# Transposing a block's rows further ahead, and two one-bank accumulators, in a fused FFT convolution and two-layer mixture kernel

## The chip, the cores and the metric

One Trainium2 chip; the kernel uses 1 of its cores. The metric is device time in microseconds (us) for one execution. Before the change the median of 3 runs is 4191.43 us (4187.36 to 4192.93).

## What is computed

Three stages on 8 x 3072 tokens of width 256, all in float32 on the host:

```
Y   = rfft(x, axis=1) * (filt_r + 1j*filt_i)           # convolution by FFT
x1  = irfft(Y)                                          # (24576, 256)
e   = argmax(x1 @ w_gate)  ;  g = softmax(...)[e]       # 8 experts, one per token
x2  = g * (relu(x1 @ w1[e]) @ w2[e])                    # w1: 256x1024, w2: 1024x256
h   = x2 @ w_in                                         # 256 -> 2048
out = piecewise(h) @ w_out                              # 0 below -1, (h+1)^2/4 between, h above 1
```

## The kernel before, in words

**Stages.** `Conv` computes the convolution and the routing in the first 640 us or so. `Ffn` computes both dense layers from there to the end, and its first blocks overlap the tail of `Conv`. Only `Ffn` and `slots` are touched by the change.

**Blocks and chunks.** Tokens are sorted by expert into blocks: 41 wide ones of 512 tokens (`NW`) and 17 narrow ones of 256 tokens that always run (up to `SURE` = 58). A block j has 8 steps `("b", j, f)`, one for each 128 columns of the expert's hidden layer. The second layer works on 48 chunks of 512 tokens; a chunk c has 16 steps `("c", c, f)`. `Ffn.run` (L1006) writes all steps into one list. It begins with 60 b steps alone (`lead`, L1012), that is blocks 0 to 6 and half of block 7. After that each chunk's 16 c steps are mixed with the next 8 b steps, the second half of one wide block and the first half of the next; in every second chunk the 8 steps of a narrow block stand between those two halves (L1017), and then c and b steps alternate one by one. Two chunks together make one period of the schedule.

**Order of the work.** `play` (L1062) walks through the list. At step i it issues the first matmuls of the step (`b_in` L870 into a bank h, or `c_in` L936), then what was put into `fill` for i, then the rest of the step's elementwise work, then what was put into `todo` for i + 1, and then the second matmuls of the step that stands 3 places earlier (`LAG` = 3: `b_out` L885 into the accumulator y, or `c_out` L964 into o). Every engine executes its own instructions in the order in which they are issued, so a waiting instruction holds all that stands behind it on its engine.

A c step is a chain over four engines: six matmuls on PE (L936), a clamp on DVE (L940), a square on ACT (L941), a sum on DVE (L943), a cast on ACT (L944, the high part gh) and a subtraction on POOL (L786, the low part gl). `c_out` three steps later needs gh, and from its third matmul on gl. A b step has ACT hh (L872) and DVE hl (L874), and two weight parts wh (ACT, L790) and wl (L786, on DVE for even f, on POOL for odd f).

**How a block gets its rows.** `plan` (L1061) sets for block j, with p[0] the place of its first step in the list: at p[0] - 26 the token numbers are fetched (`gather(j, False)`, L833, tiles ids or idl), at p[0] - 17 the rows (`gather(j, True)`, L840, 4 indirect DMAs on POOL's queue for a wide block, 2 for a narrow one; tiles row, 8 buffers), at p[0] - 9 the rows are scaled by the gate (`scale`, L847, DVE). At p[0] - 7 and p[0] - 4 the two halves (k = 0, 1) of the 256 columns are transposed by PE:

```
for k in range(2):
    at(i - 7 + 3 * k, lambda k=k: self.take(j, k, i - 6 + 3 * k))
```

`take` (L851) writes four 128 x 128 transposes (L858; two for a narrow block) into one bank. In the first blocks that bank comes from the rotating banks h (`h_tile`); once `dense` has run it is the single bank xt (`psx`, one buffer). `halves` then splits the bank: ACT copies it to xh one step later (L790), and DVE subtracts to xl (L786) as `fill` of the step after that. The two tiles xh and xl have 2 buffers each (`xp`), one for each block in work.

**The accumulator.** `b_out` at f = 0 takes a tile y of two banks from a pool with one buffer (`ps_y`) and adds into half d = 0, then d = 1. After f = 7 `b_end` (L892) empties it: for each half an ACT copy to cyh (L898) and a DVE subtraction to cyl (L899). The next block's `b_out` at f = 0 needs the same tile.

`slots` (L627) computes the block table in three phases; phases 1 and 2 run beside the first b steps and take one PSUM bank each, which is xt (`ffn.psx`, passed by the caller).

Of the kernel before, what the change touches and what calls it, by code (L numbers as in the profile page):

```python
# [9 lines left out]
FP32 = mybir.dt.float32  # L10
# [4 lines left out]
ALU = mybir.AluOpType  # L15
AX = mybir.AxisListType
PSUM = bass.MemoryType.PSUM
# [9 lines left out]
CH = 512  # L27
# [87 lines left out]
def width(j):  # L115

    return CH if j < NW else CH // 2
# [506 lines left out]
            yield t  # L624


def slots(tc, a, st, phase, pp=None, side=None):  # L627

    nc, V = tc.nc, tc.nc.vector
    nb, j0, j1 = ((EARLY, 0, NE1), (NB, NE1, NW), (NB, NW, NBLK))[phase]
    J, K, W = j1 - j0, nb - 1, width(j0)
    H, sh = W // 128, W.bit_length() - 1
    whole = phase < 2
    with ExitStack() as ctx:
        p = ctx.enter_context(tc.tile_pool(name="b", bufs=1, side=side))
        cum, off, used = st["cum"], st["off"], st["used"]
        NQ = 2 * K + 4
# [20 lines left out]
            out=out[:, 1:9], data0=one[:, 0:8], data1=x, initial=0.0, op0=ALU.mult, op1=ALU.add  # L660
# [39 lines left out]
        for k in range(2):  # L700
# [3 lines left out]
            out=QJ, in0=QT[:].unsqueeze(2).to_broadcast([8, NQ, J]), in1=oh[:, 0:1].to_broadcast([8, NQ, J]), op=ALU.mult  # L704
        )
        yield
        qs = p.tile([128, NQ, J], FP32, name="qs")
        pp = pp or ctx.enter_context(tc.tile_pool(name="b_ps", bufs=1, space=PSUM, side=side))
        ps = pp.tile([128, CH], FP32, name="xt")[:, : NQ * J].rearrange("p (q j) -> p q j", j=J)
        nc.tensor.matmul(ps, one[:8], QJ, start=True, stop=True)  # L710
        nc.scalar.copy(qs, ps)
        yield
# [4 lines left out]
            out=ecf[:, 1], in0=ecf[:, 1], scalar1=float(CH * (j0 if whole else NW)), scalar2=float(NTOK),  # L717
# [5 lines left out]
        x = p.tile([128, J, H], FP32, name="x")  # L723
        t = p.tile([128, J, H], FP32, name="t")
# [13 lines left out]
class Ffn:  # L738
# [54 lines left out]
    def at(self, i, fn, when=None):  # L793
        (self.todo if when is None else when).setdefault(max(i, self.now), []).append(fn)
# [82 lines left out]
    def b_out(self, j, f):  # L877
        nc, n = self.nc, width(j)
        (hi, lo), (wh, wl) = self.H.pop((j, f)), self.W.pop((j, f))
        if f == 0:  # L880
            self.ACC["b"] = self.ps_y.tile([128, 2, CH], FP32, name="y1")
        acc = self.ACC["b"][:, :, :n]
        for d in range(2):
            for i, (w, x) in enumerate(((wh, hi), (wh, lo), (wl, hi))):
                nc.tensor.matmul(  # L885
                    acc[:, d, :], w[:, 2 + d, :], x,
                    start=(f == 0 and i == 0), stop=(f == 7 and i == 2), skip_group_check=True,
                )
        if f == 7:
            self.b_end(j, acc, n)  # L890

    def b_end(self, j, acc, n):  # L892

        nc, a = self.nc, self.a
        pool = self.cyp if j < NW else self.y1p
        hi, lo = (pool.tile([128, 2, n], F32R, name=x) for x in ("cyh", "cyl"))
        for k in range(2):
            nc.scalar.copy(hi[:, k], acc[:, k])  # L898
            nc.vector.tensor_tensor(out=lo[:, k], in0=acc[:, k], in1=hi[:, k].bitcast(FP32), op=ALU.subtract)  # L899
        if LEADERS <= j < NW:  # L900
            self.CY[j] = (hi, lo, self.rows(self.IDS.pop(j)))
            return
        if j < NW:
            c = slice(CH * j, CH * j + CH)
        else:
            c = nc.sync.value_load(self.st["ec"][0:1, 1, j : j + 1], min_val=0, max_val=NTOK)
            c = bass.ds(c, n)
            ids = self.IDS.pop(j)
            nc.sync.dma_start(a["idc"][c].rearrange("(h p) o -> p (h o)", p=128), ids[:, :2, 0])
        for y, t in (("y1h", hi), ("y1l", lo)):  # L910
            nc.sync.dma_start(a[y][:, :, c], t[:].bitcast(FP32))
# [94 lines left out]
    def run(self):  # L1006
        self.now = -self.LEAD
        sure = SURE
        chunks = [*range(LEADERS, NW), *range(LEADERS), *range(NW, self.nch)]
        wide = [("b", j, f) for j in range(NW) for f in range(8)]  # L1010
        narrow = [[("b", j, f) for f in range(8)] for j in range(NW, sure)]
        lead = 8 * LEADERS + 12  # L1012
        steps, wide = wide[:lead], wide[lead:]
        for m, c in enumerate(chunks):
            more, wide = wide[:8], wide[8:]
            if m >= 2 and m % 2 == 0 and narrow:
                more[4:4] = narrow.pop(0)  # L1017
            n = max(8, len(more))
            for f in range(16):
                steps += [("c", c, f), *more[f * n // 16 : (f + 1) * n // 16]]  # L1020
        assert not wide and not narrow
        pos = {x: i for i, x in enumerate(steps)}
        at = self.at
        fork = pos["c", self.nch - 3, 5]
        at(fork - 16, self.load_used)

        for c in range(self.nch):
            if c < LEADERS or c >= NW:
                at(pos["c", c, 0] - 7, lambda c=c: self.load_c(c))
            for t in range(4 if c < self.nch - 1 else 0):  # L1030
                at(pos["c", c, 15] + 2 + self.LAG + t, lambda c=c, t=t: self.scatter(c, t))
        for j in range(sure):
            p = [pos["b", j, f] for f in range(8)]
            if j <= LEADERS + 1:
                self.plan(p, j, soon=j == 0)
            else:
                self.plan(p, j, ahead=6, lead=8)
        for i in range(16):
            at(lead - 12 + 2 * i, lambda i=i: self.load_w2(i))

        for i in self.play(steps):
            if i == fork:
                self.rest(sure)
            yield i
# [13 lines left out]
                pass  # L1058
        self.todo, self.fill, self.now = keep

    def plan(self, p, j, ahead=3, lead=4, soon=0):  # L1061

        at, i = self.at, p[0] - soon
        at(p[0] - 26, lambda: self.gather(j, False))
        at(p[0] - 17, lambda: self.gather(j, True))
        at(i - 9, lambda: self.scale(j))
        for k in range(2):
            at(i - 7 + 3 * k, lambda k=k: self.take(j, k, i - 6 + 3 * k))
        for q in range(4):
            at(p[2 * q] - ahead - lead, lambda q=q: self.load_w(j, q))  # L1070
        for f in range(8):
            at(p[f] - ahead, lambda f=f: self.split_w(j, f, p[f] - ahead))
# [33 lines left out]
@with_exitstack  # L1106
def tile_fftconv_moe_moe(ctx: ExitStack, tc: tile.TileContext, a: dict):
    st_p = ctx.enter_context(tc.tile_pool(name="st", bufs=1))
    st = {
        "ident": st_p.tile([128, 128], FP32, name="ident"),  # L1110
        "cum": st_p.tile([128, 9, 8], FP32, name="cum"),
        "off": st_p.tile([128, 8, 8], FP32, name="off"),
        "idx": st_p.tile([128, NSC], I32, name="idx"),
        "ec": st_p.tile([1, 2, NBLK], I32, name="ec"),
        "used": st_p.tile([128, 8], FP32, name="used"),
    }
    with tc.manual_schedule(), ExitStack() as end:
        with ExitStack() as c:
            conv = Conv(c, tc, a, st).run()
            for t in conv:  # L1120
                if t == NB * 16 - 1:
                    break
            early = slots(tc, a, st, 0, side="right")
            for t in conv:
                next(early, None)
                if t == NB * 16 + 10:
                    break
            for _ in early:
                pass
            next(conv)  # L1130
            ffn = Ffn(end, tc, a, st)
            blocks = ffn.run()
            for t in conv:
                i = next(blocks)
                for _ in range(3):
                    if i < 0:
                        i = next(blocks)
        ffn.dense(end)
        for k in (1, 2):
            for _ in slots(tc, a, st, k, ffn.psx):  # L1140
                next(blocks)
        for _ in blocks:
            pass
# [59 lines left out]
```

## Time and profile before

| | |
|---|---|
| runs | 4191.43 us median of 3 (4187.36 to 4192.93) |
| profiled execution | 4179.17 us, its span 4177.4 us |
| mean granted TensorE clock | 0.981 of full speed |
| PE busy | 3937.2 us, 94% of the span, 23852 matmuls |
| DVE, ACT, POOL busy | 55%, 48%, 56% |
| DMA | mean 87 GB/s |

PE is busy through nearly the whole span; the other three engines are busy for about half of it. A busy PE time is modelled from the starts of its matmuls, so a wait is seen best in the idle time in front of an instruction, which a row gives in brackets with the instruction that ended it. "PE xt L858 <- DVE xl L786" reads: a matmul of line 858 that writes tile xt stood idle until a DVE instruction of line 786 that writes tile xl ended.

### The profile page before, as it was taken

How to read it: one execution, taken by the hardware profiler on the slowest of the kernel's cores; microseconds unless marked ns; L12 is line 12 of the kernel's file. 1: busy time of each engine (PE TensorE's matmuls, PEld its weight loads, DVE VectorE, ACT ScalarE, POOL GpSimd, SP SyncE). 2: the span in 40 equal slices, each digit the busy share in tenths (PEclk: the TensorE clock that was granted, in tenths of full speed). 3: DMA queues.
4: the chain of work that ended last, by engine and by line, in shares of the span. 5: the costliest groups of instructions: out<-in, count | busy, mean ns of one | idle time of the engine just before them, and what ended most of it. 6: DMA issues, size and time to landing. Idle time of an engine off the chain costs nothing. (4 is left out here: it accounts for less than half of the span.)

```text
span 4177.4 us, 63452 instructions
## 1 busy us (share of the span) xinstructions
PE 3937.2 (94%) x23852; PEld 3345.2 (80%) x23852; DVE 2280.7 (55%) x3643; ACT 2020.2 (48%) x3625; POOL 2334.2 (56%) x2202
## 2 busy tenths in 40 slices
PE   8988887899999999999999999999999999999999
PEld 5655655678888888888888888888888888888888
DVE  5899985564444444444444444444544544454444
ACT  4765664444444444444444444444444444444444
POOL 5777765435555555555555555555555455555555
PEclk9999988999999999999999999999999999999999
DMA  9877764341211211111212111111121121111110
GB/s 298 255 215 220 219 195 132 128 142 56 64 59 56 64 59 58 62 59 60 65 54 64 61 59 60 60 60 60 59 64 59 56 64 39 36 41 35 33 32 26
DMA packets 239321, 364.05 MB, mean 87 GB/s; under 512 B 36544, under 2 KB 160736, under 8 KB 239008
## 3 DMA queue, kind: packets, MB, share of 16 engines
q1 hardware_dynamic: 205280, 300.09, 23.2%
q0 software_dynamic: 25056, 51.36, 4.1%
q10 hardware_dynamic: 8672, 8.48, 0.7%
q8 instruction: 190, 3.11, 0.3%
q14 instruction: 123, 1.01, 0.1%
HBM read 260.52 MB, written 99.30 MB: 86 GB/s over the span
## 5 line engine op out<-in xcount | busy, mean ns | idle before, releaser
L786 POOL TENSOR_TENSOR gl<-m,gh 128x512 fp32r<-128x512 f32 x768 | 997.6, 1299 | 1407.8 <-ACT gh L944 883.2
L941 ACT ACTIVATE m<-m,half 128x512 f32<-128x512 f32 x768 | 556.7, 725 | 1083.3 <-DVE m L940 1083.1
L964 PE MATMUL o<-woh,gh 128*128 128x256 f32 x3084 | 879.5, 285 | 8.1 <-ACT os L957 7.9
L964 PE MATMUL o<-wol,gh 128*128 128x256 f32 x3084 | 871.8, 283 | 1.2 <-DMA wol<-s_w2s 1.2
L964 PE MATMUL o<-woh,gl 128*128 128x256 f32 x3084 | 870.6, 282 | 0.0
L940 DVE TENSOR_SCALAR m<-h 128x512 f32<-128x512 f32 x768 | 529.6, 690 | 520.0 <-PE h L936 456.4
L943 DVE SCALAR_TENSOR_TENSOR m<-h,m 128x512 f32<-128x512 f32 x768 | 530.7, 691 | 487.1 <-ACT m L941 487.1
L944 ACT CAST gh<-m 128x512 fp32r<-128x512 f32 x768 | 476.2, 620 | 606.1 <-DVE m L943 605.3
L874 DVE SCALAR_TENSOR_TENSOR hl<-h,hh 128x512 fp32r<-128x512 f32 (+1 forms) x464 | 284.2, 612 | 661.1 <-ACT hh L872 659.8
L964 PEld LDWEIGHTS o<-woh,gh 128*128 128x128 f32 x3084 | 586.8, 190 | 38.8 <-ACT os L957 12.6
L964 PEld LDWEIGHTS o<-wol,gh 128*128 128x128 f32 x3084 | 588.3, 191 | 27.1 <-DMA wol<-s_w2s 1.5
L936 PE MATMUL h<-cyh,winh 128*128 128x512 f32 x1536 | 608.4, 396 | 1.0 <-PEq L1052 1.0
L936 PE MATMUL h<-cyl,winh 128*128 128x512 f32 x1536 | 606.6, 395 | 0.0
L936 PE MATMUL h<-cyh,winl 128*128 128x512 f32 x1536 | 605.0, 394 | 0.0
L964 PEld LDWEIGHTS o<-woh,gl 128*128 128x128 f32 x3084 | 587.9, 191 | 0.0
L885 PE MATMUL y<-hh,wh 128*128 128x512 f32 (+1 forms) x928 | 343.4, 370 | 21.4 <-DVE cyl L899 21.4
L786 POOL TENSOR_TENSOR wl<-raw,wh 128x512 fp32r<-128x512 f32 x232 | 303.7, 1310 | 96.0 <-ACT wh L790 85.0
L870 PE MATMUL h<-xh,wh 128*128 128x512 f32 (+1 forms) x928 | 341.7, 368 | 5.1 <-DVE hl L874 4.1
L936 PEld LDWEIGHTS h<-cyh,winl 128*128 128x128 f32 x1536 | 289.1, 188 | 67.8
L870 PE MATMUL h<-xh,wl 128*128 128x512 f32 (+1 forms) x928 | 338.2, 364 | 5.1 <-POOL wl L786 4.6
L870 PE MATMUL h<-xl,wh 128*128 128x512 f32 (+1 forms) x928 | 337.6, 364 | 0.0
L885 PE MATMUL y<-hh,wl 128*128 128x512 f32 (+1 forms) x928 | 337.2, 363 | 0.0
(193 smaller groups left out, 6423.7 us busy)
## 6 DMA issues: line engine op xcount, KB each, us to landing
raw<-in_w_dram SPq DMA_DIRECT2D x232, 512.0 KB, 3.4
f<-in_filt_dram SPq DMA_DIRECT2D x72, 384.0 KB, 4.8
xt<-in_x_dram SPq DMA_DIRECT2D x64, 384.0 KB, 5.6
s_z<-zs SPq DMA_DIRECT2D x128, 192.0 KB, 3.7
zt<-s_z SPq DMA_DIRECT2D x64, 384.0 KB, 5.2
s_y<-y SPq DMA_DIRECT2D x128, 192.0 KB, 5.1
cyh<-s_y1h SPq DMA_DIRECT2D x13, 512.0 KB, 3.9
cyl<-s_y1l SPq DMA_DIRECT2D x13, 512.0 KB, 5.1
```

What stands on the lines that cost most here:

```text
L786: eng.tensor_tensor(out=lo, in0=src, in1=hi.bitcast(FP32), op=ALU.subtract)
L870: nc.tensor.matmul(o, w[:, k, :], x[:, k, :], start=i == 0, stop=i == 5)
L874: nc.vector.scalar_tensor_tensor(out=lo, in0=o, scalar=0.0, in1=hi.bitcast(FP32), op0=ALU.max, op1=ALU.subtract)
L885: nc.tensor.matmul(acc[:, d, :], w[:, 2 + d, :], x, start=(f == 0 and i == 0), stop=(f == 7 and i == 2), skip_group_check=True,)
L936: nc.tensor.matmul(ps, w[:, k, 128 * f : 128 * f + 128], x[:, k, :], start=n == 0, stop=n == 5)
L940: V.tensor_scalar(out=m, in0=ps, scalar1=-1.0, scalar2=1.0, op0=ALU.max, op1=ALU.min)
L941: nc.scalar.activation(m, m, ACTF.Square, bias=self.half[:, 0:1], scale=-0.5)
L943: V.scalar_tensor_tensor(out=m, in0=ps, scalar=-1.0, in1=m, op0=ALU.max, op1=ALU.add)
L944: nc.scalar.copy(hi, m)
L964: self.nc.tensor.matmul(self.ACC["c"][t // 2][:, t % 2, :], x[:, 128 * t : 128 * t + 128], w[:, f, :], start=(f == 0 and t % 2 == 0 and n ...
```

## The change

Four edits. (1) `plan` gets a parameter `early`. Blocks 8 and later (up to the last sure one) get (13, 11, 6): rows are gathered at p[0] - 20, scaled at p[0] - 13, and the two halves transposed at p[0] - 11 and p[0] - 6. Blocks 0 to 7 get the default (9, 7, 4), which is what they had, but for the gather of rows, which comes at p[0] - 16 in place of p[0] - 17. (2) The accumulator y becomes two tiles of one bank each. (3) In chunks with a narrow block an empty slot stands before and after the narrow block's 8 steps; the chunk's 18 slots are spread over its 16 c steps, and empty ones are left out. (4) `slots` takes its bank in phases 1 and 2 from the rotating banks h in place of xt.

```diff
-def slots(tc, a, st, phase, pp=None, side=None):
+def slots(tc, a, st, phase, bank=None, side=None):
...
-        pp = pp or ctx.enter_context(tc.tile_pool(name="b_ps", bufs=1, space=PSUM, side=side))
-        ps = pp.tile([128, CH], FP32, name="xt")[:, : NQ * J].rearrange("p (q j) -> p q j", j=J)
+        if not bank:
+            pp = ctx.enter_context(tc.tile_pool(name="b_ps", bufs=1, space=PSUM, side=side))
+            bank = lambda: pp.tile([128, CH], FP32, name="q")
+        ps = bank()[:, : NQ * J].rearrange("p (q j) -> p q j", j=J)
...
         if f == 0:
-            self.ACC["b"] = self.ps_y.tile([128, 2, CH], FP32, name="y1")
-        acc = self.ACC["b"][:, :, :n]
+            self.ACC["b"] = [self.ps_y.tile([128, CH], FP32, name=f"y{d}") for d in range(2)]
+        acc = [t[:, :n] for t in self.ACC["b"]]
...
-                    acc[:, d, :], w[:, 2 + d, :], x,
+                    acc[d], w[:, 2 + d, :], x,
...
         for k in range(2):
-            nc.scalar.copy(hi[:, k], acc[:, k])
-            nc.vector.tensor_tensor(out=lo[:, k], in0=acc[:, k], in1=hi[:, k].bitcast(FP32), op=ALU.subtract)
+            nc.scalar.copy(hi[:, k], acc[k])
+            nc.vector.tensor_tensor(out=lo[:, k], in0=acc[k], in1=hi[:, k].bitcast(FP32), op=ALU.subtract)
...
             if m >= 2 and m % 2 == 0 and narrow:
-                more[4:4] = narrow.pop(0)
+                more[4:4] = [None, *narrow.pop(0), None]
             n = max(8, len(more))
             for f in range(16):
-                steps += [("c", c, f), *more[f * n // 16 : (f + 1) * n // 16]]
+                steps += [("c", c, f), *filter(None, more[f * n // 16 : (f + 1) * n // 16])]
...
-                self.plan(p, j, ahead=6, lead=8)
+                self.plan(p, j, ahead=6, lead=8, early=(13, 11, 6))
...
-    def plan(self, p, j, ahead=3, lead=4, soon=0):
+    def plan(self, p, j, ahead=3, lead=4, soon=0, early=(9, 7, 4)):
         at, i = self.at, p[0] - soon
         at(p[0] - 26, lambda: self.gather(j, False))
-        at(p[0] - 17, lambda: self.gather(j, True))
-        at(i - 9, lambda: self.scale(j))
+        at(p[0] - early[0] - 7, lambda: self.gather(j, True))
+        at(i - early[0], lambda: self.scale(j))
         for k in range(2):
-            at(i - 7 + 3 * k, lambda k=k: self.take(j, k, i - 6 + 3 * k))
+            at(i - early[1 + k], lambda k=k: self.take(j, k, i - early[1 + k] + 1))
...
-            for _ in slots(tc, a, st, k, ffn.psx):
+            for _ in slots(tc, a, st, k, ffn.h_tile):
                 next(blocks)
```

## Rows read from the trace of the kernel before

**Rows 1.** The page: busy us of each engine, share of the span, instructions
```profile
PE 3937.2 (94%) x23852; PEld 3345.2 (80%) x23852; DVE 2280.7 (55%) x3643; ACT 2020.2 (48%) x3625; POOL 2334.2 (56%) x2202
```

**Rows 2.** Waits of PE from 900 us on: us in total, times, longest us
```profile
PE xt L858 <- DVE xl L786: 78.7, 50, 2.8
PE y L885 <- DVE cyl L899: 18.8, 16, 1.2
```

**Rows 3.** Timeline around one second transpose: start us, us, engine, line, operation, [idle before]
```profile
1506.52 0.40 PE L936 MATMUL h<-cyl,winh 128*128 128x512 f32 x1
1506.75 0.39 PE L936 MATMUL h<-cyh,winl 128*128 128x512 f32 x1
...
1507.25 0.69 DVE L940 TENSOR_SCALAR m<-h 128x512 f32<-128x512 f32 x1 [0.73 <-POOL gap L1004]
...
1507.86 0.41 DVE L786 TENSOR_TENSOR xl<-xt,xh 128x256 fp32r<-128x256 f32 x1
...
1508.33 0.44 PE L858 MATMUL xt<-ident,row 128*128 128x128 f32 x2 [1.19 <-DVE xl L786]
```

**Rows 4.** Windows of 3.4 us from a second transpose on: engines' busy us, granted clock
```profile
1083.27:1086.67 3.40, 3.40 (x17) 3.40 (x18) 1.07 (x2) 1.14 (x3) 2.77 (x4) 0.51 0.05 1
...
1239.53:1242.93 3.40, 3.40 (x20) 3.40 (x21) 1.11 (x3) 1.59 (x5) 2.77 (x4) 0.62 0.02 1
...
1395.76:1399.16 3.40, 3.40 (x29) 3.40 (x30) 1.50 (x3) 1.91 (x5) 2.77 (x4) 1.00 0.04 1
...
1550.46:1553.86 3.40, 3.40 (x18) 3.40 (x19) 1.08 (x2) 1.32 (x4) 2.78 (x4) 0.57 0.04 1
...
3499.94:3503.34 3.40, 3.40 (x15) 3.32 (x16) 2.13 (x2) 0.90 (x2) 1.41 (x2) 0.51 0.02 5
```

**Rows 5.** Timeline where a narrow block takes the accumulator after a wide one
```profile
1528.80 0.69 DVE L899 TENSOR_TENSOR cyl<-y,cyh 128x512 fp32r<-128x512 f32 x1 [1.69 <-ACT cyh L898]
...
1530.15 0.69 DVE L899 TENSOR_TENSOR cyl<-y,cyh 128x512 fp32r<-128x512 f32 x1 [0.65 <-ACT cyh L898]
...
1530.89 0.38 PE L885 MATMUL y<-hh,wh 128*128 128x256 f32 x1 [1.17 <-DVE cyl L899]
```

**Rows 6.** Waits of PE from 600 to 900 us
```profile
PE y L885 <- DVE cyl L899: 2.6, 2, 1.4
```

**Rows 7.** Timeline at the first block, POOL and PE
```profile
661.74 0.94 POOL L840 DMA_INDIRECT row<-s_y,idl  x1 [0.30 <-issue]
...
666.45 2.49 POOL L786 TENSOR_TENSOR wl<-raw,wh 128x512 fp32r<-128x512 f32 x2
...
667.77 0.80 PE L870 MATMUL h<-xh,wl 128*128 128x512 f32 x1 [4.59 <-POOL wl L786]
```

**Rows 8.** Timeline of three c steps beside a narrow block, PE and POOL
```profile
1539.25 0.40 PE L936 MATMUL h<-cyh,winl 128*128 128x512 f32 x1
...
1540.91 0.60 PE L858 MATMUL xt<-ident,row 128*128 128x128 f32 x4
...
1545.82 0.28 PE L964 MATMUL o<-woh,gl 128*128 128x256 f32 x1
...
1548.19 0.39 PE L936 MATMUL h<-cyh,winl 128*128 128x512 f32 x1
...
1552.71 0.94 POOL L833 DMA_INDIRECT ids<-s_L,idx  x1 [0.30 <-PE y L885]
1553.66 1.29 POOL L786 TENSOR_TENSOR gl<-m,gh 128x512 fp32r<-128x512 f32 x1
```

**Rows 9.** Timeline of a burst of row gathers beside a wide block, POOL and PE
```profile
1517.36 1.29 POOL L786 TENSOR_TENSOR gl<-m,gh 128x512 fp32r<-128x512 f32 x1 [2.09 <-ACT gh L944]
...
1518.81 0.98 POOL L840 DMA_INDIRECT row<-s_y,ids  x1 [0.15 <-issue]
...
1522.07 0.28 PE L964 MATMUL o<-woh,gl 128*128 128x256 f32 x1
1522.61 0.95 POOL L840 DMA_INDIRECT row<-s_y,ids  x1 [0.30 <-issue]
```

## The prediction, made before the changed kernel was run

> **What bounds the kernel now.** I read the page first: PE is busy for 94% of the span, the other engines for about half [rows 1]. From the end of the convolution on, time can therefore come from two places only: fewer or shorter matmuls, which this change doesn't bring, or the moments in which PE stands idle. So the second view is PE's list of waits. From 900 us on it is nearly empty but for two lines [rows 2]: 50 waits of the transposes in `take` for a DVE subtraction into xl, 78.7 us together, and 16 waits of `b_out` for the subtraction into cyl, 18.8 us. Fifty is the number of blocks from 8 to 57: every such block waits once.
>
> The timeline around one of them shows why [rows 3]. The waiting transposes are the second half (k = 1) of a block. They write the one bank xt, which the first half still holds until DVE has subtracted xl. That subtraction is issued as `fill` two steps after the first transposes, behind the clamp (L940) of a c step, and the second transposes are issued right behind that same c step's matmuls. So PE ends the matmuls and then waits for the clamp (0.69 us) and for xl, which both need these very matmuls or stand behind them. It is a wait by order, not by load.
>
> The wait costs more than the bracket says. In front of it the matmuls start 0.23 us apart (1506.52, 1506.75); the next would have started at 1506.98 and started at 1508.33, so 1.35 us are lost where the bracket says 1.19: 0.16 us more [rows 3].
>
> A second price is the clock. [...] The low windows all follow the longest of the waits. What one costs can be read from the period of the schedule: from 1239.53 (a low one) to the next such point at 1395.76 it takes 156.23 us, from 1395.76 (clock 1.00) to 1550.46 it takes 154.70, so 1.5 us [rows 4]. [...]
>
> **The change part by part**, against the profiled execution of 4179.17 us (span 4177.4; it lies 12.3 us under the median of the runs, and I subtract the gain from the median).
>
> *Transposes 11 and 6 steps ahead.* Now the ACT copy comes at p - 10, the DVE subtraction at p - 9, and the second transposes at p - 6, three steps later in place of behind the same step. A pair of steps takes over 4 us of PE, and DVE is late by about one chain. The wait goes in full: 78.7 + 50 x 0.16 = 86.7 us. What comes next in its place? The first transposes need xt from the block before, released at that block's p - 4; blocks follow each other by 16 steps or more, so no wait there. X has two buffers, and the copies at p - 10 reuse that of the block two before, whose last step lies before the previous block's first, so 6 steps or more back. Rows are held from p - 20 to p - 6, 14 steps against 13: 8 buffers hold two wide blocks, and a gather reuses rows whose transposes are done. The scale keeps its 2 steps ahead of the first transposes, the gather its 7 ahead of the scale. SP's queue gets nothing new. Blocks 0 to 7 keep their places and their waits.
>
> *Clock.* With the long waits gone the clock has no reason to fall behind them: 11 x 1.53 = 16.8 us. Between 0 (it falls for another reason) and 16.8 I take all of it, since after the waits that are shorter, and after some of the long ones (1395.76), it stays at 1.00 [rows 4].
>
> *Free slots and the split accumulator.* The 16 waits sit where a narrow block follows a wide one: one c step stands between `b_out` at f = 7 and at f = 0, and the emptying of y (two subtractions, 1528.80 to 1530.84) ends just in front of the narrow block's first matmul at 1530.89 [rows 5]. With the slot, one more c step (18 matmuls) is put there; six at 0.23 us alone are 1.4 us, more than the wait. So it goes: 18.8 + 16 x 0.16 = 21.4 us, the 0.16 being an estimate from the transposes. The slot adds no instruction; it puts two b steps side by side elsewhere. In the slot's presence the split into two tiles has little left to do; without slots, in the b-only stretch, it frees half 0 one subtraction earlier. The two waits there are 2.6 us [rows 6]; between 0 and 2.6 I take 1.
>
> *Gather one step later for blocks 0 to 7.* This is the default (9, 7, 4). On POOL's queue block 2's four row gathers now stand in front of block 0's weight subtraction wl for f = 1, which then starts at 666.45, and PE waits 4.6 us for it [rows 7]. One step later they stand behind it: wl can start at about 661.74, where the first gather did. Between a loss of 1.3 (the gathers wait for that wl) and a gain of 4.6 I take 4, since the rows aren't needed for many steps.
>
> *Slots in a bank h.* Two calls in the whole kernel, four matmuls. Nothing, hidden by the rotation of three banks; should it show, a wait like the shortest here, about 1 us.
>
> *What is late next.* In the narrow stretch the lo part gl of a c step is what PE could meet. A step without a gather in its way has, from the end of its matmuls (1539.65) to the first matmul that needs gl (1545.82), 6.17 us, of which up to 0.60 are transposes that now stand elsewhere. Where the four fetches of token numbers of the next wide block stand on POOL in front of gl, the chain takes from 1548.58 to 1554.95, 6.37 us [rows 8]. Today the long wait behind this step covers that; without it PE is late by 0.2 to 0.8 us, once in each of 16 periods. I take 0.5: 8 us given back. The row gathers move from p - 17 to p - 20. A burst of four is 4 x (0.95 + 0.30) = 5.0 us on POOL. At its new place it pushes the gl that started at 1517.36 with POOL idle 2.09 us in front, so by 2.9 us, where gl has 3.42 us of room (1518.65 to 1522.07) and the slot adds more [rows 9]: nothing, with an upper bound of 16 x 2.9 = 46 us if that room weren't there.
>
> **Sum**: 86.7 + 16.8 + 21.4 + 1 + 4 - 8 = 121.9 us. The profiled execution would become 4057 us, the median 4191.4 - 121.9 = 4069.5, said as 4069.
>
> **The rivals.**
> *The waits come back as waits for gl.* The stalls in the narrow stretch (about 1.3 us of y and 2 us of the transposes behind it) sit inside the room of several c steps, and so gave POOL time. If PE then meets gl late by as much, 16 x 3.3 and the clock's 16.8 are given back, 70 us: 4139. For it: the room there is thin [rows 8]. Against it: POOL is busy for 56% of the span [rows 1], and a c step with no burst in front has its whole chain done in time today. 8%.
> *The change doesn't do what it says*: xt is still held when the second half comes, because ACT or DVE work of the other steps stands in front at the new place as it did at the old. Then only y and the first stretch gain, 21.4 + 5 = 26: 4165. Against it: two full steps of PE work now lie between subtraction and transposes. 5%.
> *Slower by bursts on POOL.* Every wide block from 8 on (33) puts its four row gathers at a new place. If the gl behind each is late by the whole 5.0 us, that is 165 us against a gain of 130 (the sum without the 8): 4191.4 - 130 + 165 = 4226. It decides from 130 / 33 = 3.9 us per block on. Against it: the burst lands three steps earlier, in the wide stretch, with the room named above [rows 9]. 3%.
>
> **How the numbers follow.** The forecast has 84%. Its own range: all terms at their best and nothing given back, 86.7 + 16.8 + 21.4 + 2.6 + 4.6 = 132.1, is 4059; executions lie up to 12.3 us under the median, so 4050. At the worst, 2 us late in each of the 16 periods (32 in place of 8) and nothing from the two early terms, it is 121.9 - 24 - 5 = 93, 4098, and 4105 with the same scatter. What is left out are the three rivals, 16%. About 0.2% (8 us) is what a measurement of this kernel can tell from no change. Faster by more: forecast and the first two rivals, less a little for mixtures of the third, 95%; within it 2%; slower 3%.
>
> **What would show it right or wrong.** In the new profile the line of xt waiting for xl should keep one wait or two (block 7, about 3 us), y for cyl at most two; no window between 900 and 3500 us should have a clock under 1.00; a period should take about 149 us; a new line, PE o waiting for POOL gl, should stay under 10 us. If that line holds tens of us, the first rival is right; if xt still waits some fifty times, the second.

## The result and the profile after

The changed kernel takes 4060.23 us (median of 4 runs, 4059.17 to 4060.95), the kernel before 4191.23 (4 runs): ratio 0.9689, 95% interval 0.9672 to 0.9705, that is 131.0 us less. The forecast was 4069, in a range of 4050 to 4105. The profiled execution took 4060.95 us, its span 4059.1.

The page's busy line answers to [rows 1], and the list of PE's waits from 900 us on (us in total, times, longest us) to [rows 2]:

```profile
PE 3906.9 (96%) x23852; PEld 3330.0 (82%) x23852; DVE 2311.7 (57%) x3643; ACT 2006.7 (49%) x3625; POOL 2354.4 (58%) x2202
...
PE o L966 <- ACT os L959: 11.5, 13, 2.3
PE o L966 <- POOL gl L788: 6.8, 15, 1.0
PE o L966 <- DMA wol<-s_w2s: 1.3, 1, 1.3
```

The matmuls are as many as before; what went is idle time. Both lines of [rows 2] are gone, xt for xl (78.7 us) and y for cyl (18.8). The top line, o for os, is for 11 of its waits the kernel's tail, where the output is emptied; these were there before, with 7.9 us. Two more, of 1.2 and 2.3 us around the last narrow block (at 3396 and 3455 us), came with the free slots, since the kernels without them have 11 such waits and none over 1.0. The new line is the one forecast, o waiting for POOL's gl.

The timeline at one of the 15 gl waits answers to [rows 8], with the first matmuls of the same wait one period before and after:

```profile
1372.93 0.38 PE L966 MATMUL o<-woh,gl 128*128 128x256 f32 x1 [0.42 <-POOL gl L788]
...
1517.67 1.35 POOL L835 DMA_INDIRECT ids<-s_L,idx  x1 [0.30 <-issue]
1519.33 0.94 POOL L835 DMA_INDIRECT ids<-s_L,idx  x1 [0.30 <-issue]
1520.29 1.31 POOL L788 TENSOR_TENSOR gl<-m,gh 128x512 fp32r<-128x512 f32 x1
1521.65 0.38 PE L966 MATMUL o<-woh,gl 128*128 128x256 f32 x1 [0.42 <-POOL gl L788]
...
1670.37 0.39 PE L966 MATMUL o<-woh,gl 128*128 128x256 f32 x1 [0.42 <-POOL gl L788]
```

POOL is in the middle of the four fetches of token numbers when the c step's gl is due, and PE is late by 0.42 us. The distance of the three waits is the period: 148.72 us, against 154.70 and 156.23 before [rows 4]. The two periods as windows (us, then busy us of PE, PEld, DVE, ACT, POOL, the granted clock, DMA share, GB/s), with two stretches of 500 us that can be set beside the kernel before, whose rows stand second:

```profile
1372.93:1521.65 148.72, 148.30 (x885) 131.21 (x885) 77.61 (x125) 71.44 (x126) 85.62 (x80) 1.00 0.21 63
1521.65:1670.37 148.72, 148.30 (x884) 131.22 (x884) 77.62 (x125) 71.33 (x126) 85.60 (x80) 1.00 0.22 63
...
1000.00:1500.00 500.00, 498.75 (x2965) 440.83 (x2964) 260.67 (x415) 239.74 (x424) 289.21 (x273) 1.00 0.21 63
1500.00:2000.00 500.00, 498.32 (x2989) 441.63 (x2988) 261.53 (x423) 240.02 (x426) 286.52 (x266) 1.00 0.22 63
```

```profile
1000.00:1500.00 500.00, 482.65 (x2843) 424.30 (x2842) 242.43 (x398) 233.72 (x407) 271.02 (x256) 0.99 0.19 59
1500.00:2000.00 500.00, 480.29 (x2829) 421.72 (x2828) 241.65 (x398) 230.47 (x404) 272.19 (x261) 0.99 0.19 61
```

PE idles 0.42 us of a period, and the granted clock is 1.00 throughout: no window between 900 and 3500 us is lower, where before 11 of the 50 second transposes were followed by a low one, of 0.51 to 0.69 [rows 4].

Where the 131 us lie: from the first c step's first matmul to the last matmul it took 3288.5 us before (884.3 to 4172.8) and 3177.4 after (877.2 to 4054.5). These are 111.1 us, where the terms of the forecast for this stretch (86.7, 16.8, 21.4, less 8) make 116.9. The rest, 7.1 us, lies ahead of the first c step, and it is the balance of two larger numbers. From the first matmul of a b step to the first c step it took 226.1 us before (from 658.1) and 203.0 after (from 674.2): 23.1 us less, where the forecast has 5. But the first b step begins 16.1 us later. There the profiled executions are not alike: in the one after, PE stands idle at 640 to 664 us in a way that the one before lacks (waits of PE from 600 to 900 us, after):

```profile
PE i L327 <- issue: 15.9, 2, 10.8
PE h L860 <- DVE xl L788: 6.3, 4, 1.9
...
PE h L872 <- DVE hl L876: 2.4, 4, 1.5
PE xt L860 <- DVE xl L788: 2.4, 1, 2.4
```

The first line's matmuls belong to the convolution, whose lines are not edited; what holds them up the profile doesn't name. The two profiles differ by 118.2 us and the runs by 131.0, and the profiled execution of before lay 12 us under its median. If the other runs of before have this idling too, that is the difference; this is argued, not shown. The waits for wl [rows 7] and for y [rows 6] are gone.

### The profile page after: what moved, and what is told of

Same layout as the page of the kernel before. It is cut to its first block, busy times and chain, and to the rows that moved or that the text cites. A ratio compares the mean times of both kernels' runs of the same rounds, so it can differ in the third digit from the quotient of the medians.

```text
span 4059.1 us, 63531 instructions
## 1 busy us (share of the span) xinstructions
PE 3906.9 (96%) x23852; PEld 3330.0 (82%) x23852; DVE 2311.7 (57%) x3643; ACT 2006.7 (49%) x3625; POOL 2354.4 (58%) x2202
## 5 line engine op out<-in xcount | busy, mean ns | idle before, releaser
L788 POOL TENSOR_TENSOR wl<-raw,wh 128x512 fp32r<-128x512 f32 x232 | 303.4, 1308 | 92.3 <-ACT wh L792 86.7
L872 PE MATMUL h<-xh,wh 128*128 128x512 f32 (+1 forms) x928 | 337.2, 363 | 5.0 <-DVE hl L876 2.4
L872 PE MATMUL h<-xh,wl 128*128 128x512 f32 (+1 forms) x928 | 334.2, 360 | 0.0
L872 PE MATMUL h<-xl,wh 128*128 128x512 f32 (+1 forms) x928 | 333.7, 360 | 0.0
```

What stands on the lines that cost most here:

```text
L788: eng.tensor_tensor(out=lo, in0=src, in1=hi.bitcast(FP32), op=ALU.subtract)
L872: nc.tensor.matmul(o, w[:, k, :], x[:, k, :], start=i == 0, stop=i == 5)
```

## The experiments

Three batches, each beside runs of the kernel before on the same chip: 4176.3 us beside the first, 4189.0 beside the second, 4190.1 beside the third. Times are compared within a batch or by ratio; the third batch holds no run of the changed kernel, so there a comparison with it is one across batches.

**One part alone, and nothing.** Each kernel is the kernel before with one edit of the change.

*The moved transposes alone*, with the slots' bank from h, which has to go with them, since xt is now held for longer (neither was tried without the other); blocks 0 to 7 stay as they were:

```diff
-                self.plan(p, j, ahead=6, lead=8)
+                self.plan(p, j, ahead=6, lead=8, early=(13, 11, 6))
...
-    def plan(self, p, j, ahead=3, lead=4, soon=0):
+    def plan(self, p, j, ahead=3, lead=4, soon=0, early=(10, 7, 4)):
```

> Only the earlier places of rows, scale and transposes for blocks 8 and later, with the bank of the block table taken from the rotating banks (which these places need); accumulator, free slots and the first blocks' gather as before. Theory (the second transposes waited by order alone, and the long waits pulled the clock down): the line xt waiting for xl loses its 50 waits, no slow stretch of the clock is left after 900 us, the 16 waits of y for cyl stay at about 18 us, and PE meets gl late by under 10 us in total; 100 us less than before, 4080 to 4100 us. Rival (the waits come back as waits for gl): xt is quiet, but PE o waits for POOL gl by 40 us or more, about 4140 us. Rival (the slow clock hangs on something else): the eleven slow stretches stay, about 4107 us.

Measured: 4107.38 us, ratio 0.9835 (0.9819 to 0.9852), 69 us less. Its waits of PE from 900 us on:

```profile
PE o L966 <- POOL gl L788: 25.0, 31, 1.5
PE y L887 <- DVE cyl L901: 18.8, 16, 1.2
```

xt for xl is gone and y stays to the tenth, as forecast. But gl takes 25.0 us in 31 waits: two per period, where the whole change has one. So part of the first rival is true of this part alone. 86.7 + 16.8 - 25.0 = 78.5, less 0.16 us more per wait (5), is 73.5, near the 69.

*The free slots alone*:

```diff
-                more[4:4] = narrow.pop(0)
+                more[4:4] = [None, *narrow.pop(0), None]
```

(and the empty slots left out of the list of steps).

> Only the free slots before and after a narrow block's steps. Theory: the 16 waits of y for cyl go and nothing else, 21 us less, about 4170 us; the 50 waits of xt stay. Rival (one more c step is not enough in front of the accumulator, the split is what frees it): y keeps half or more of its waits, 4180 us or more.

Measured: 4135.19, ratio 0.9899 (0.9883 to 0.9916), 41 us less: far more than expected. y's waits are gone; of xt's, those of all narrow blocks but the last are gone too, and the longest of each period is down from 1.88 to 1.61 us, at the cost of waits for gl:

```profile
PE xt L858 <- DVE xl L786: 54.1, 34, 2.2
PE o L964 <- POOL gl L786: 12.3, 16, 0.8
```

Behind none of the 32 waits of xt in the periods is the clock low. It is low once between 900 and 3500 us, behind the first wait (2.19 us, at 911).

*The split accumulator alone*:

```diff
-            self.ACC["b"] = self.ps_y.tile([128, 2, CH], FP32, name="y1")
+            self.ACC["b"] = [self.ps_y.tile([128, CH], FP32, name=f"y{d}") for d in range(2)]
```

(with the four uses of it).

> Only the accumulator as two tiles of one bank each. The trace of the changed kernel shows the two ACT copies of the emptying back to back, where before the second one waited 0.76 us for DVE. Theory now: that wait was for the tile of two banks; without it each emptying is about 0.65 us shorter, so the 16 waits of y shrink by about that, 10 us, and the stretch of b steps alone (up to 900 us) gets shorter by some 10 us more through the subtractions that stand behind it; about 4171 us. Rival (as forecast: only half 0 comes free one subtraction earlier, 1 to 3 us): about 4189 us.

Measured: 4131.68, ratio 0.9895 (0.9878 to 0.9911), 45 us less. The waits of y are gone without any slot, and in the 16 periods the clock stays up, though xt still waits 76.0 us in 49 waits. The same second transposes as in [rows 4], in this kernel: the stall, and the windows of 3.4 us behind it in two periods (last three numbers: clock, DMA share, GB/s):

```profile
1528.87 0.30 PE L858 MATMUL xt<-ident,row 128*128 128x128 f32 x1 [1.89 <-DVE xl L786]
...
1528.93:1532.33 3.40, 3.40 (x29) 3.40 (x30) 1.43 (x3) 1.90 (x4) 2.77 (x4) 1.00 0.05 1
1375.32:1378.72 3.40, 3.40 (x29) 3.40 (x30) 1.46 (x3) 1.90 (x4) 2.77 (x4) 1.00 0.05 1
```

In the kernel before, this wait is in its brackets as long, and there the clock falls behind it:

```profile
1550.46 0.41 PE L858 MATMUL xt<-ident,row 128*128 128x128 f32 x2 [1.88 <-DVE xl L786]
```

There the clock is low behind 10 of the 16 waits of this place (16 periods), here behind none. What PE meets ahead of it in the kernel before, and not here, is y's wait 20 us earlier (1530.89, [rows 5]). It is tempting to say that the low clock needs both waits, but this same kernel has two longer waits of xt, outside the periods and with no wait for y ahead of them, and behind both the clock fell (0.53 and 0.51 over 3.4 us):

```profile
899.11 1.09 PE L858 MATMUL xt<-ident,row 128*128 128x128 f32 x4 [2.17 <-DVE xl L786]
3452.14 0.66 PE L858 MATMUL xt<-ident,row 128*128 128x128 f32 x2 [2.06 <-DVE xl L786]
...
899.11:902.51 3.40, 3.40 (x17) 3.40 (x18) 1.57 (x5) 0.63 (x2) 1.27 (x1) 0.53 0.45 113
3452.14:3455.54 3.40, 3.40 (x15) 3.35 (x16) 2.14 (x2) 0.90 (x2) 1.41 (x2) 0.51 0.02 5
```

The traces' records of the granted clock show another difference. In the profiles of the kernel before and of the changed kernel they hold two values alone, 1.00 and 0.50 of full speed. All the clock's changes in a profile lie on one even beat, of 3.413 us in these two, to within 0.01 us. In the two profiles of the kernel before, 20 of the 32 waits of this place are followed by a low clock, and all 20 begin 0.15 to 1.45 us after a point of that beat; the other 12 begin elsewhere on it, two of them 0.01 us after a point. With the split alone these waits come 153.6 us apart each time (154.70 or 156.23 in the kernel before), all 16 between 0.02 and 0.04 us after a point of the beat: one case, met 16 times. So in these profiles whether the clock falls behind a wait of 1.88 us goes with the moment at which the wait begins. The split moved that moment, which is luck as far as these runs show. With slots alone the waits of 1.61 and 1.54 us begin all over the beat and none is followed by a low clock; with the transposes moved, no such wait is left. So any one of the three parts takes the low clock of the periods away, but not for the same reason. Whether y's wait plays a part as well isn't shown.

*The kernel before, again*:

> The kernel before, unchanged, for a second profile of the stretch from 635 to 665 us, in which the changed kernel's profile has all engines idle for some 20 us with nothing named to wait for and the first profile of before has not. If that idling belongs to the program at this place, it shows here too and explains why the profiled execution of before lay 12 us under its other runs: a span of about 4190 us. If it belongs to the changed kernel, it is absent and the span is again about 4177 us.

Measured: 4174.99, ratio 0.9995 (0.9986 to 1.0005). No idling at 640 to 664 us, 12 low clock windows. Its first c step begins at 877.6 us; with the split alone at 868.8, with slots alone at 880.8, with the transposes alone at 880.2. In all four the first b step begins at 652.7 to 653.5. The split is what shortens the stretch of b steps, by 9 us.

Alone, the parts give 69, 41 and 45 us, together 155; the whole change gives 131. They overlap in the clock (16.8, in each of the three), in y's waits (21.4, in two of them) and in xt's (24.6 us of them go with the slots alone, all with the transposes), and slots and transposes meet at gl.

**One part less, and less distance.** These start from the changed kernel.

> The changed kernel itself, beside the same runs of before as the next three. The median of before on this chip is about 4176 us, so at the measured ratio 4046 us. In the first profile of it all engines idled for some 20 us between 637 and 664 us with nothing to wait for. If that idling belongs to the program, it shows again at that place; if it belongs to one execution or one chip, it is gone, the first b step starts near 653 us as in the three other profiles of this chip, and the span is some 15 us shorter than the ratio says.

Measured: 4058.98, ratio 0.9685 (0.9669 to 0.9702). The idling at 640 to 664 us is there again, so it belongs to more than one execution. Whether it goes with the chip or with the program isn't shown: in all nine profiles of the changed kernel and its variants the first b step begins at 664 to 674 us, in all five of the kernel before and of one part alone at 653 to 658, and no kernel was profiled with it and without it.

This profile differs from the first in one point that bears on the clock: the wait for os near 3455 us, as long in both, is followed by a low clock here, and by the full clock there (the first profile's window stands second):

```profile
3455.19:3458.59 3.40, 3.40 (x15) 3.15 (x16) 0.69 (x2) 1.34 (x2) 2.00 (x2) 0.61 0.70 211
```

```profile
3455.29:3458.69 3.40, 3.40 (x22) 3.13 (x23) 0.89 (x3) 1.34 (x2) 2.01 (x2) 1.00 0.71 230
```

The wait is 2.34 us in both. The sign that the forecast named, no low window between 900 and 3500 us, so holds in one of the two profiles.

*Without the split* (the accumulator is one tile of two banks again):

> The changed kernel with the accumulator as one tile of two banks again. Theory (either the free slot or the split removes the waits of y beside narrow blocks, the split alone also shortens the stretch of b steps): no wait of y for cyl after 900 us, a period of the schedule as in the changed kernel, 148.7 us, and 9 to 12 us more in the stretch up to 900 us; 10 us slower than the changed kernel. Rival (the forecast's small term for the split): 1 to 3 us slower.

Measured: 4083.72, ratio 0.9745 (0.9729 to 0.9761), 25 us slower than the changed kernel. No wait for y comes back after 900 us, and gl stays at 6.8 in 15 waits; yet the period is 149.50 us in place of 148.72. One new line of waits stands in the list, small in itself:

```profile
PE xt L860 <- DVE row L849: 2.8, 15, 0.2
```

The timeline of the emptying of y and what stands behind it, in this kernel (one fence) and in the changed kernel (the second):

```profile
1509.23 0.59 ACT L900 CAST cyh<-y 128x512 fp32r<-128x512 f32 x1 [0.76 <-DVE cyl L901]
...
1509.84 0.69 DVE L901 TENSOR_TENSOR cyl<-y,cyh 128x512 fp32r<-128x512 f32 x1 [0.65 <-ACT cyh L900]
...
1513.93 1.65 DVE L849 TENSOR_SCALAR row<-row,ids 128x256 f32<-128x256 f32 x4
...
1514.93 1.02 PE L860 MATMUL xt<-ident,row 128*128 128x128 f32 x4
```

```profile
1494.77 1.08 ACT L900 CAST cyh<-y 128x512 fp32r<-128x512 f32 x2
...
1495.39 1.29 DVE L901 TENSOR_TENSOR cyl<-y,cyh 128x512 fp32r<-128x512 f32 x2 [0.57 <-ACT cyh L900]
...
1500.07 1.65 DVE L849 TENSOR_SCALAR row<-row,ids 128x256 f32<-128x256 f32 x4
...
1501.58 0.60 PE L860 MATMUL xt<-ident,row 128*128 128x128 f32 x4
```

Here is what the split does. With one tile, ACT's copy of the second half waits 0.76 us for DVE's subtraction of the first, though both read only, and DVE then waits 0.65 us for ACT. With two tiles the copies run back to back, and so do the subtractions. What stands behind the emptying on DVE then comes earlier, here the scaling of rows: it begins 4.68 us after the first subtraction (1495.39 to 1500.07) in place of 5.43 (1508.50 to 1513.93). Without the split its four parts run into the transposes, which take 1.02 us in place of 0.60. A comparison of all matmul starts over 14 periods puts 10.8 of the 10.9 us at these transposes and in front of them. Of the 25 us, 9 to 10 lie ahead of the first c step (886.1 against 877.2 and, on this chip, 876.6); counted from the first b matmul it is 12 (214.7 against 202.5 on this chip). Another 12.5 lie in 16 periods, 0.78 in each. These 12.5 us are no gain over the kernel before, which has no wait of xt for row after 900 us: they come with the new place of the transposes, and the split takes them away again.

In the changed kernel ACT reads y (until 1495.85) while DVE reads it too (from 1495.39), 0.46 us side by side. All that the edit changes is one tile or two, so the 0.76 us go with the single tile; by what way it brings them these runs don't show.

*Without the slots*:

> The changed kernel without the free slots. Theory (the split already removes the waits of y, and the slots' share is the room for gl): no wait of y for cyl, but PE o waits for POOL gl by about 25 us over some 31 waits as in the kernel with the transposes moved alone, against 6.8 us over 15; with the two longer waits for ACT os at the last narrow block gone (3.6 us), 10 to 18 us slower than the changed kernel. Rival (the slots remove the waits of y): y waits again, 20 us and more slower.

Measured: 4091.46, ratio 0.9765 (0.9749 to 0.9782), 32 us slower than the changed kernel. y doesn't wait; the price is gl, 29.6 us in 31 waits, against 6.8 in 15. The second wait per period is at the burst of [rows 9], POOL's and PE's timeline:

```profile
1642.73 0.95 POOL L842 DMA_INDIRECT row<-s_y,ids  x1 [0.30 <-issue]
1643.98 1.01 POOL L998 DMA_INDIRECT out_dram<-os,ids  x1 [0.30 <-issue]
...
1645.04 1.31 POOL L788 TENSOR_TENSOR wl<-raw,wh 128x512 fp32r<-128x512 f32 x1
1646.30 1.27 POOL L788 TENSOR_TENSOR gl<-m,gh 128x512 fp32r<-128x512 f32 x1
1647.63 0.39 PE L966 MATMUL o<-woh,gl 128*128 128x256 f32 x1 [1.00 <-POOL gl L788]
```

The row gathers at their new place, with an output scatter and a wl behind them, do push a gl past its room, unless the slot adds some. With the split in place, giving POOL that room is what the slots are for, not y.

*Halves three steps apart, not five* (the first half two steps later):

```diff
-                self.plan(p, j, ahead=6, lead=8, early=(13, 11, 6))
+                self.plan(p, j, ahead=6, lead=8, early=(13, 9, 6))
```

> The changed kernel with the first half's transposes 9 instead of 11 steps ahead, the second half's still 6: three steps apart, as before the change, but both further ahead of the block than before. Theory (what counts is the distance between the two halves, because the subtraction that frees the bank is issued in the very step whose matmuls stand in front of the second transposes): xt waits for xl again, over at least 34 waits with 54 us as in the kernel with the slots alone, so about 60 us slower than the changed kernel; the clock stays at its upper level. Rival (what counts is the place, ahead of the block's own weight work): less than 10 us slower, xt quiet.

Measured: 4108.19, ratio 0.9804 (0.9787 to 0.982), 49 us slower than the changed kernel. xt waits for xl again, with no wait for gl and the clock up:

```profile
PE xt L860 <- DVE xl L788: 52.0, 33, 1.6
```

For the wide blocks the distance between the halves is what removes the wait. Of the 33, 32 are theirs, two in each of 16 periods. Of the narrow blocks only the last still waits, as with the slots alone; the others don't wait at three steps either.

**Four tries around the changed kernel.**

*Blocks 0 to 7 gather 17 steps ahead again*:

```diff
-        at(p[0] - early[0] - 7, lambda: self.gather(j, True))
+        at(p[0] - early[0] - 7 - (early[0] == 9), lambda: self.gather(j, True))
```

> The changed kernel with one thing put back: blocks 0 to 7 gather their rows 17 steps ahead again, not 16. My theory (the 4 us of the sum): the b weight part wl of the first b steps stands behind four row gathers on POOL again, PE waits about 4.6 us for it, and the time is about 4 us over the changed kernel's 4060, so 4064. Rival: PE stands idle at 640 to 664 us anyway, the wl is early enough beside that, and the time stays within 1 us of 4060. In either case no other line of waits moves.

Measured: 4067.00, ratio 0.9706 (0.9689 to 0.9722), some 7 us more than the changed kernel, whose interval from another batch (0.9672 to 0.9705) overlaps with this one. From the first b matmul to the first c step it takes 209.9 us against 203.0; the first c step comes at 882.1 against 877.2. PE doesn't wait for wl; it waits longer for hl (h L872 for hl: 6.6 us in 9 waits, against 2.4 in 4, and h L860 for hl 2.2 us more). So the size of the term is about right, as far as a comparison across batches can tell, and its place isn't: neither theory holds. Beside the idling at 640 to 664 us, which this kernel has too, wl is early enough; without that idling the term wasn't measured. Why hl is late was not found.

*Token numbers of blocks 8 and on fetched 38 steps ahead*:

```diff
-        at(p[0] - 26, lambda: self.gather(j, False))
+        at(p[0] - (26 if j <= LEADERS + 1 else 38), lambda: self.gather(j, False))
```

> The changed kernel with the token numbers of blocks 8 and on fetched 38 steps ahead instead of 26, so that the four fetches on POOL don't stand in front of that gl. My theory (the 8 us given back are POOL's order, not its load): the line o waits for gl, 6.8 us in 15 waits, falls under 2 us, the period falls from 148.7 by about 0.55 us, and the time is 4051 to 4053. Rival: POOL is simply late by then, the same gl or the next one stays late, gl keeps 5 us or more and the time stays at 4060.

Measured: 4074.02, ratio 0.9727 (0.9714 to 0.9741), 14 us slower than the changed kernel's 4060: both theories miss. gl waits 22.1 us in 15 waits, and the period is 149.79. POOL's timeline in front of one of them, with the matmul that waits:

```profile
1187.02 0.95 POOL L842 DMA_INDIRECT row<-s_y,ids  x1 [0.30 <-issue]
1187.99 1.30 POOL L788 TENSOR_TENSOR gl<-m,gh 128x512 fp32r<-128x512 f32 x1
1189.24 1.29 POOL L788 TENSOR_TENSOR wl<-raw,wh 128x512 fp32r<-128x512 f32 x1
1190.68 0.95 POOL L835 DMA_INDIRECT ids<-s_L,idx  x1 [0.16 <-issue]
...
1195.41 2.52 POOL L788 TENSOR_TENSOR gl<-m,gh 128x512 fp32r<-128x512 f32 x2
...
1196.74 0.39 PE L966 MATMUL o<-woh,gl 128*128 128x256 f32 x1 [1.47 <-POOL gl L788]
```

The fetches now follow right behind another block's four row gathers and two output scatters, and POOL has no pause over 0.31 us from 1179.2 to 1199.2. Their first place was the better one.

*Halves of the first blocks four steps apart*, at 8 and 4 steps ahead:

```diff
-    def plan(self, p, j, ahead=3, lead=4, soon=0, early=(9, 7, 4)):
+    def plan(self, p, j, ahead=3, lead=4, soon=0, early=(10, 8, 4)):
```

> The changed kernel with the halves of blocks 0 to 7 transposed four steps apart (two copies more of distance: transposes 10 and 6 steps ahead in the early argument 10, 8, 4), so that the early blocks get what the change gave the later ones. Theory: the waits for xl between 600 and 900 us (6.3 us of h and 2.4 of xt behind it) shrink by half or more and the time is about 4 to 6 us less, 4054 to 4056. Rival: there the emptying of x and h on DVE is the bound (b steps only, no c steps between), so the waits stand elsewhere and the time stays within 2 us of 4060.

Measured: 4058.94, ratio 0.9686 (0.9670 to 0.9702): within 2 us of the changed kernel. The waits for xl (6.3 and 2.4 us) are gone entirely, and hl for h takes 6.7 us in 6 waits, against 2.4 in 4, so half comes back. Against the changed kernel the rival's number is right, its reason isn't shown: the edit also scales these rows and gathers them one step earlier, 17 steps ahead as in the first of these four tries. Beside that one, on the same chip and with the same place of the gather, it is 8.1 us faster (4058.94 against 4067.00), and the stretch from the first b matmul to the first c step takes 200.7 us against 209.9. So the distance, with the earlier scale, gains about what the gather's place costs; with the gather at 16 it wasn't tried.

*Both of these edits, the later fetch and the distance in the first blocks:*

> Both of the two edits before together. They touch different stretches (600 to 900 us, and from 900 us on), so what they gain should add: by the theories 4046 to 4049; if only the later fetch holds, 4052; if neither, 4060.

Measured: 4071.87, ratio 0.9726 (0.9711 to 0.9741), as the later of its two edits alone. No version beat the changed kernel by more than can be measured.

## Why the prediction was right, and where its sizes were off

The mechanism held as written: PE's waits were an order, and distance removes them. By the steps:

- *Transposes, 86.7 us*: right. The 50 waits became one, block 7's (2.4 us). With three steps between the halves 52.0 us of waits return, so for the wide blocks it is the distance. But the term wasn't free by itself: alone it gives back 25.0 us at gl, and without the split the transposes at their new place meet the scaling of rows, 12.5 us. "The scale keeps its 2 steps ahead of the first transposes" left that out.
- *Clock, 16.8 us*: the low windows behind xt's waits are gone, as forecast, and with the transposes moved alone they are gone too. In the trace of before 11 of 50 windows were low (0.51 to 0.69), and the 1.53 us of each was read from two of its periods (156.23 less 154.70); no run shows the product, 16.8, by itself. The slots alone or the split alone end them as well in the periods, the one by shorter waits and the other by the moment at which they begin, so the term can't be put down to one part. Nor does the length of the wait in front decide alone: one of 1.88 us is followed by a low clock in 20 of 32 cases, and one of 2.34 us in one profile of two.
- *y's waits, 21.4 us*: right. The slots alone remove the 16 waits, as forecast, and so does the split alone: either is enough.
- *The split, taken as 1 of 0 to 2.6 us*: this is the step that failed, in the words "In the slot's presence the split into two tiles has little left to do". With the slots in place its lack costs 25 us, and none of that is a wait for y after 900 us. In the b-only stretch it measures 9 us (877.6 to 868.8 with it alone) to 12 (214.7 to 202.5 with the rest), and in the c steps 0.78 us per period. The row on which the term went, [rows 6], counts PE's direct waits for y. What the shared tile cost besides was, in the trace of before, 0.65 us of DVE's queue at each of the 41 emptyings of a wide block and 0.44 at each of the 17 of a narrow one, handed on to row and whatever else stands behind it.
- *The gather of the first blocks, 4 us*: about 7 in its stretch and in the runs, by a comparison across batches that isn't clear of noise, and not by way of wl.
- *gl, 8 us given back*: 6.8, at the fetches of token numbers, as derived from [rows 8].
- *Row gathers at their new place, nothing, "and the slot adds more"*: right; without the slots it costs a wait per period.

The sum was 121.9 and the runs gave 131.0, only 9.1 more, and that closeness is in part luck, since larger misses cancel. The c steps gave 111.1 us in place of 116.9. The b steps ahead of them gave 23.1 in place of 5: of these 18 more, 8 to 11 are the split and about 3 the gather; the rest wasn't taken apart. The first b step begins 16.1 us later in the profile after; the medians take back 12.8 of these, by the idling that is argued for the other runs of before. The ends of the range are also a few us narrower than their working gives: 4059 less 12.3 is 4047, 4098 and 12.3 are 4110. The measured time lies well inside either.

Of the rivals, waits coming back as gl was the nearest: it is true of the transposes alone (25.0 us) and of the change without slots (29.6), and the slots are what kept it small.

## What to carry to other kernels

When two engines empty a buffer half by half, look for a short wait of one reader for the other (here 0.76 us of ACT and 0.65 of DVE): here a tile per half removed it, and with the slots in place the gain of 25 us was found in whatever stands behind it on the slower engine's queue, not in the waits for the buffer. Price parts that remove the same wait, or the same slow clock, once; test each alone and each left out before crediting one. An outcome counted 16 times in a schedule with a fixed period can be one case met 16 times. Before a burst is moved on a queue, its new neighbours should be counted: four fetches moved twelve steps away from one tight place landed behind six other DMA issues and cost 14 us, where 7 to 9 were to be saved.

## What was not expected of the hardware

In these profiles the granted clock's answer to a wait of about 2 us goes with when the wait begins. Behind waits of 1.88 us in the kernel before it fell, to 0.51 to 0.70 over 3.4 us, in 20 of 32 cases in two profiles, and the 20 are told from the others by their place on the beat, of 3.413 us, on which all of the clock's changes lie. The same program, with the same wait of 2.34 us at the same place, kept the full clock in one profile of the changed kernel and fell to 0.61 in the other. Waits of 1.61 us, 16 of them spread over the beat with the slots alone, brought it down in no case. And near 650 us PE idles for 8.1 to 15.0 us at a stretch in all nine profiles of the changed kernel and its variants (10.8 in the first, which the profile puts down to issue), and in none of the five others; whether the chip or the program brings it, and what ends it, the records don't show.
